# Attention values moved behind the MLP piece, and probability copies moved to the next step

## The chip, the cores and the metric

The kernel runs on one core of a Trainium2 chip. The metric is the time of one execution on the device, in microseconds (us). Below, PE is the matrix engine, PEld its weight loads, DVE the vector engine, ACT the scalar engine, POOL the GpSimd engine and SP the engine that issues most transfers. Each engine gets its own list of instructions in the order of the program; between engines, semaphores make a reader wait for its writer and a writer wait until a buffer is free.

## The reference

An attention of 2 batches, 8 heads, 768 positions and head size 64, in which a query sees four sink positions and a window of 128, is followed by two MLPs (512 to 2048 to 512) over the 1536 tokens:

```python
scores = scale * np.matmul(q, k.transpose(0, 1, 3, 2))
keep = is_sink | in_window
scores = np.where(keep, scores, -1000000000.0)
a = np.exp(scores - np.max(scores, axis=-1, keepdims=True))
a = a / (np.sum(a, axis=-1, keepdims=True) + 1e-09)
x = np.matmul(a, v)                       # heads joined to 512 columns
h = x @ w_in                              # first MLP
g = np.where(h > 0.0, h, alpha * (np.exp(np.minimum(h, 0.0)) - 1.0))
x = g @ w_out
h = x @ w_in2                             # second MLP
g = np.maximum(h, 0.0) + alpha2 * np.minimum(h, 0.0)
out = g @ w_out2
```

## The kernel before, in words

**Attention in steps.** The queries of a batch are cut into seven blocks of 110 (the last has 108). A unit is one or two blocks of one pair of heads; there are 32 units, and the loop `for s in range(nu + 2)` in `fast_path` runs 34 steps. A unit passes through three of them. In step s PE makes the scores of unit s (`scores`, line 521, tiles qk); DVE adds the mask and finds the maximum (line 529), ACT makes the exponentials (line 534), DVE the reciprocals of their sums (lines 544 and 547, tile st), and POOL multiplies by them (line 551, `normalised`). In the same step PE transposes the probabilities of unit s-1 (`transposed`, line 565, tiles t in PSUM), which DVE copies into SBUF (line 649, tiles pt; up to step 9 ACT copies the second block of a unit). And PE multiplies the values with the transposed probabilities of unit s-2 (`values`, line 586, tile x); ACT rounds the result to its high part xh (line 594), and DVE makes the remainder xl (line 596). xh and xl are the input of the first MLP.

**MLP pieces between.** All MLP products are made of three matmuls on high and low parts (`matmul3`, line 293). While attention runs, PE also takes one MLP piece a step from the list `fill`: an h piece (`g1`, 12 matmuls into one PSUM tile, evicted by two ACT operations at lines 325 and 326 and one DVE operation at 327, tile u; in the next step ACT makes gh at line 339 and POOL gl at line 340) or an o piece (`g2`, 12 matmuls, evicted by one ACT copy at line 359). The pieces have 220, 220, 328 and 440 columns; 32 of them are in the list, each with the first step at which it may run (`at_`). Where a step has no piece, two groups of four dummy matmuls (`keep_busy`, line 251, tile busy) stand in its place. What is left of the list runs after the loop.

**Weights.** Eight weight halves are decoded during attention, in the steps of `DS` (1, 3, 5, 7, 9, 10, 11, 12): two ACT operations (lines 267 and 268) at the end of the step before, four DVE operations (lines 270, 273, 276, 279) in the step, and one of ACT (line 283, wh) and one of DVE (line 285, wl) in the step after.

**Order.** Inside the loop the program sets the order by hand (`manual_schedule`): each engine gets its instructions in the order in which the Python code issues them. The tiles t, x, h, o and busy share four PSUM buffers (pool `ps`), taken in turn; qk has four of its own.

After the loop comes `mlp_rounds`, which does the rest of both MLPs with larger pieces.

Of the kernel before, what the change touches and what calls it, by code (L numbers as in the profile page):

```python
# [34 lines left out]
HP = H // 2  # L35
# [21 lines left out]
DS = [1, 3, 5, 7, 9, 10, 11, 12]  # L57
# [56 lines left out]
def attention_mlp2(  # L114
# [13 lines left out]
    nc = tc.nc  # L128
# [45 lines left out]
    def load_v(g, pool=None):  # L174
        b, z, hp = sgs[g]
        n = VCH[z] * 2 * D
        if pool:
            t = pool.tile([P, max(VCH) * 2 * D], F32, tag="vr", name=f"vr{g}", bufs=LB)
        else:
            t = room[:, HP * 2 * KTOT[0] + g * n :]  # L180
        nc.sync.dma_start(out=t[:, :n], in_=vc[b, hp, :, V0[z] : V0[z] + n])
        vals[g] = t
# [10 lines left out]
    def load_w(m, fc, io, raw=None):  # L193
        if raw is None:
            raw = rawp.tile([P, DM, 2], I32, tag="raw", name=f"wr{m}_{fc}_{io}")
        nc.sync.dma_start(
            out=raw, in_=weights[m][fc, io].bitcast(I32).rearrange("p (n t) -> p n t", t=2)
        )
        wraw[m, fc, io] = raw
# [18 lines left out]
    for i, most in enumerate((SINK, 0, WIN, 0)):  # L218
# [7 lines left out]
        out=flag_i, in0=int1[:, 2:3].bitcast(U32), scalar=0.5, in1=flag_m, op0=ALU.is_ge, op1=ALU.mult  # L226
# [6 lines left out]
        out=lims, in0=intf[:, :, 0], scalar=0.0, in1=intf[:, :, 1], op0=ALU.is_lt, op1=ALU.add  # L233
    )
    nc.vector.scalar_tensor_tensor(
        out=lims, in0=lims, scalar=4294967296.0, in1=intf[:, :, 0], op0=ALU.mult, op1=ALU.add
# [10 lines left out]
    def keep_busy(pool, tag, n):  # L247

        t = pool.tile([P, 512], F32, tag=tag, name=f"busy{next(ids)}")
        for _ in range(n):  # L250
            nc.tensor.matmul(t[:, :P], ident, ident, start=True, stop=True)  # L251
# [121 lines left out]
    def done(steps):  # L373
        for _ in steps:
            pass
# [87 lines left out]
    def make_mask(blk):  # L463
        o = sum(KW[i] for i in MASKS if i < blk)
        masks[blk] = mk = mask_t[:, o : o + KW[blk]]

        nc.vector.tensor_scalar(
            out=mk, in0=rels[blk].bitcast(U32), scalar1=win, scalar2=-NEG / SCALE,
            op0=ALU.is_ge, op1=ALU.mult,
        )  # L470

        nc.vector.scalar_tensor_tensor(
            out=mk[:, :SINK], in0=skey, scalar=ns, in1=mk[:, :SINK], op0=ALU.is_ge, op1=ALU.mult
        )
# [17 lines left out]
    def fast_path():  # L492
# [47 lines left out]
        def normalised(i):  # L540
            _, blks = units[i]
            n, c = NQ[blks[0]], len(blks)
            sb, st = soft[i]
            nc.vector.tensor_scalar(
                out=st[:n, 2, :c], in0=st[:n, 1, :c], scalar1=1.0e-9, scalar2=None, op0=ALU.add
            )
            nc.vector.reciprocal(st[:n, 3, :c], st[:n, 2, :c])  # L547
            for j, blk in enumerate(blks):
                w = KW[blk]
                for e in range(2):  # L550
                    nc.gpsimd.tensor_scalar(  # L551
                        out=sb[:n, j, e, :w], in0=sb[:n, j, e, :w], scalar1=st[:n, 3, j, e : e + 1],
                        scalar2=1.0, op0=ALU.mult, op1=ALU.mult,
                    )

        def transposed(i):
            _, blks = units[i]
            sb, _ = soft.pop(i)
            for j, blk in enumerate(blks):
                n, c, r = NQ[blk], NCH[blk], CR[blk]  # L560
                tp = ps.tile([P, 512], F32, tag="ps", name=f"t{i}_{blk}")
                for e in range(2):
                    for k in range(c):
                        o = (e * c + k) * n
                        nc.tensor.transpose(  # L565
                            tp[:r, o : o + n], sb[:n, j, e, k * r : k * r + r], ident[:n, :n]
                        )
                pt = at.tile([P, 4 * QB], F32, tag="pt", name=f"pt{i}_{blk}", bufs=PB)
                trans[i, blk] = pt
                yield pt[:r, : 2 * c * n], tp[:r, : 2 * c * n]  # L570

        def values(i):
            g, blks = units[i]
            b, z, hp = sgs[g]
            vr = vals[g]
            px = ps.tile([P, 512], F32, tag="ps", name=f"x{i}")
            o = 0
            for blk in blks:
                n, c, r = NQ[blk], NCH[blk], CR[blk]
                v0 = sum(NCH[SPLIT[z][0] : blk]) * 2 * D  # L580
                pt = trans.pop((i, blk))
                for e in range(2):
                    for k in range(c):
                        vs = v0 + (k * 2 + e) * D
                        p0 = (e * c + k) * n
                        nc.tensor.matmul(  # L586
                            px[e * D : e * D + D, o : o + n], vr[:r, vs : vs + D], pt[:r, p0 : p0 + n],
                            start=(k == 0), stop=(k == c - 1),
                        )
                o += n  # L590
            c0 = b * S + Q0[blks[0]]
            xh, xl = (x[:, hp, c0 : c0 + o] for x in xs)

            nc.scalar.copy(xh, px[:, :o])  # L594
            yield
            nc.vector.tensor_tensor(out=xl, in0=px[:, :o], in1=xh, op=ALU.subtract)  # L596


        nu = len(units)
        last_of = {g: i for i, (g, _) in enumerate(units)}  # L600
        fill = []
        first, second = [], []
        for j, (c0, n, t) in enumerate(TOK0[:-1]):
            at_ = last_of[t * HP + HP - 1] + 2
            first.append([(at_, lambda c0=c0, n=n, fc=fc: mlp.g1(0, c0, n, fc)) for fc in range(FG)])
            second.append([(at_, lambda c0=c0, n=n, d=d: mlp.g2(0, c0, n, 0, d)) for d in range(KC)])

# [15 lines left out]
        load_w(*ws[HP])  # L623
        decodes = {}
        gates = []
        for s in range(nu + 2):
            late = s - 1 in decodes
            if late:
                next(decodes[s - 1])
            for a in gates:  # L630
                done(a)
            gates = []
            if late:
                done(decodes.pop(s - 1))
            sc = scores(s) if s < nu else iter(())
            next(sc, None)
            vs = values(s - 2) if s >= 2 else iter(())
            next(vs, None)
            done(sc)
            done(vs)  # L640
            if s in decodes:
                next(decodes[s])
            take = 1 if fill and fill[0][0] <= s else 0
            after = fill.pop(0)[1]() if take else None
            if not take and s < nu:
                keep_busy(ps, "ps", BUSYN)
            if 1 <= s <= nu:
                for j, (out, in_) in enumerate(transposed(s - 1)):
                    (nc.scalar.copy if j and s <= DS[HP] else nc.vector.tensor_copy)(out, in_)  # L649
            if s < nu:  # L650
                normalised(s)
            if not take and s < nu:
                keep_busy(ps, "ps", BUSYN)
            if after:
                after = after()
                next(after)
                gates.append(after)
            if len([f for f in fill if f[0] <= s]) >= FILL_MAX:
                after = fill.pop(0)[1]()()
                next(after)  # L660
                gates.append(after)
            for blk, at_ in MS.items():
                if s == at_:
                    make_mask(blk)
            if s + 1 in DS:
                decodes[s + 1] = decode_w(at2, wa, *ws[DS.index(s + 1)])
                next(decodes[s + 1])
            if s in DS and WPRE <= DS.index(s) and DS.index(s) + 3 < len(ws):
                load_w(*ws[DS.index(s) + 3])
            if s < nu:  # L670
                g = units[s][0]
                if s == last_of[g] and HP <= g and g + LB < len(sgs):
                    load_kq(g + LB, at)
            if s >= 2:
                g = units[s - 2][0]
                if s - 2 == last_of[g] and HP <= g and g + LB < len(sgs):
                    load_v(g + LB, at)
# [97 lines left out]
    with tc.If(fast > 0) as cond:  # L775
        fast_path()
# [54 lines left out]
```

## Time and profile before

| | |
|---|---|
| Three timed runs | 662.41, 661.69 and 660.24 us, median 661.69 us |
| Profiled execution, from the first to the last instruction | 660.5 us; no time of its own is listed beside the three runs |
| Instructions | 9670 |
| Busy: PE / PEld / DVE / ACT / POOL | 633.7 / 526.6 / 435.9 / 315.7 / 204.4 us |
| Mean granted clock of PE | 0.986 |

Busy times are sums over the whole span; the loop of the attention steps fills about the first quarter of it. A row of the timeline gives the start, the duration, the engine, the line and operation, and in brackets how long the engine had been idle and for whom it waited. Rows of one engine overlap a little, since an instruction starts while the one ahead still writes; the time that an instruction takes from a busy engine is the distance from its start to the start of the next.

### The profile page before, as it was taken

What the parts mean: (1) busy time and instruction counts of PE and PEld (TensorE: products, weight loads), DVE (VectorE), ACT (ScalarE), POOL (GpSimd) and SP (SyncE); (2) the same over time, 40 slices, a digit from 0 to 9 for tenths busy, and PEclk for the clock granted to TensorE, in tenths of its full rate; (3) what the DMA queues carried; (4) which work ended last, traced back from release to release, by engine and by line L of the source; (5) the groups of instructions that cost most, each with busy time, mean ns of one, the idle gap of its engine ahead of it and who ended that gap; (6) DMA issues with size and microseconds to landing.
All of it is one profiled execution on the core that took longest, in us unless ns stands there. A gap on an engine that the chain in (4) does not pass through costs nothing.

```text
span 660.5 us, 9670 instructions
## 1 busy us (share of the span) xinstructions
PE 633.7 (96%) x3444; PEld 526.6 (80%) x3444; DVE 435.9 (66%) x927; ACT 315.7 (48%) x719; POOL 204.4 (31%) x253
## 2 busy tenths in 40 slices
PE   8986899999989899999999999999999999999996
PEld 7775688887977677888888888888888888888885
DVE  5877767655399997768465876694669673343332
ACT  4877466655588675647545733453524230110010
POOL 3354334434123321233215453332123312331130
PEclk9988799999999999999999999999999999999999
DMA  8574336500043343121112211212222000000112
GB/s 256 149 213 140 106 85 167 158 25 1 34 159 127 124 132 128 37 91 64 65 58 70 65 64 44 84 65 65 64 65 64 33 0 1 2 0 1 64 50 83
DMA packets 21659, 52.87 MB, mean 80 GB/s; under 512 B 2658, under 2 KB 9826, under 8 KB 21602
## 3 DMA queue, kind: packets, MB, share of 16 engines
q1 hardware_dynamic: 21024, 51.93, 25.8%
q8 instruction: 29, 0.48, 0.3%
q10 hardware_dynamic: 578, 0.24, 0.2%
q14 instruction: 28, 0.23, 0.1%
HBM read 49.01 MB, written 3.15 MB: 79 GB/s over the span
## 4 chain that ended last, share of the span: by engine, by line
PE 78%; DVE 13%; ACT 4%; issue 2%; POOL 1%; DMA 1%; DVEq 0%; ACTq 0%; SPq 0%; POOLq 0%
PE o L293 36%; PE h L293 34%; PE x L586 3%; DVE wx L276 3%; DVE wx L279 2%; ACT s L534 2%; PE t L565 2%; PE qk L521 2%; DVE wl L285 2%; DVE wx L273 1%; DVE wx L270 1%; DVE pt L649 1%; DVE u L327 1%; DVE acc L361 1%; PE busy L251 1%
## 5 line engine op out<-in xcount | busy, mean ns | idle before, releaser
L340 POOL TENSOR_TENSOR gl<-u,gh 128x512 fp32r<-128x512 f32 (+3 forms) x104 | 133.1, 1280 | 327.6 <-ACT gh L339 322.5
L293 PE MATMUL o<-gh,wh 128*128 128x512 f32 (+3 forms) x416 | 157.3, 380 | 5.5 <-DVE u L327 5.5
L293 PE MATMUL h<-xh,wh 128*128 128x512 f32 (+3 forms) x416 | 158.1, 380 | 1.2 <-ACT xh L594 1.2
L293 PE MATMUL o<-gl,wh 128*128 128x512 f32 (+3 forms) x416 | 156.3, 376 | 1.8 <-POOL gl L340 1.7
L293 PE MATMUL h<-xl,wh 128*128 128x512 f32 (+3 forms) x416 | 156.6, 376 | 0.1
L293 PE MATMUL h<-xh,wl 128*128 128x512 f32 (+3 forms) x416 | 156.4, 376 | 0.0
L293 PE MATMUL o<-gh,wl 128*128 128x512 f32 (+3 forms) x416 | 155.8, 375 | 0.0
L339 ACT CAST gh<-u 128x512 fp32r<-128x512 f32 (+3 forms) x104 | 60.9, 585 | 139.3 <-DVE u L335 114.2
L293 PEld LDWEIGHTS o<-gh,wh 128*128 128x128 f32 x416 | 78.4, 189 | 23.4 <-DVE u L327 8.4
L361 DVE TENSOR_TENSOR acc<-o,acc 128x512 f32<-128x512 f32 x72 | 49.2, 688 | 72.0 <-PE o L293 71.7
L293 PEld LDWEIGHTS h<-xh,wh 128*128 128x128 f32 x416 | 79.2, 190 | 16.9 <-ACT xh L594 1.3
L293 PEld LDWEIGHTS o<-gl,wh 128*128 128x128 f32 x416 | 78.8, 189 | 16.0 <-POOL gl L340 2.9
L293 PEld LDWEIGHTS h<-xl,wh 128*128 128x128 f32 x416 | 79.3, 191 | 13.6 <-DVE xl L596 0.4
L293 PEld LDWEIGHTS h<-xh,wl 128*128 128x128 f32 x416 | 79.4, 191 | 13.4
L293 PEld LDWEIGHTS o<-gh,wl 128*128 128x128 f32 x416 | 78.8, 189 | 13.5
L551 POOL TENSOR_SCALAR s<-s,st 110x250 f32<-110x250 f32 (+5 forms) x112 | 52.6, 487 | 92.3 <-DVE st L547 31.1
L283 ACT CAST wh<-wx 128x512 fp32r<-128x512 f32 x64 | 39.6, 619 | 65.6 <-DVE wx L279 31.7
L534 ACT ACTIVATE s<-s,st 110x250 f32<-110x250 f32 (+5 forms) x112 | 53.1, 477 | 27.1 <-DVE st L529 27.0
L331 DVE TENSOR_SCALAR u<-h,alpha_sb 128x512 f32<-128x512 f32 x48 | 35.9, 748 | 45.6 <-PE h L293 45.6
L279 DVE CUSTOM_DVE_ANT_0 wx<-wx,wq 128x1024 uint16<-128x1024 uint16 x64 | 59.2, 925 | 1.4
L276 DVE SCALAR_TENSOR_TENSOR wx<-wr,wx 128x512 int32<-128x512 int32 x62 | 56.6, 914 | 1.0
L285 DVE TENSOR_TENSOR wl<-wx,wh 128x512 fp32r<-128x512 f32 x64 | 46.8, 733 | 15.5 <-ACT wh L283 13.9
(56 smaller groups left out, 634.5 us busy)
## 6 DMA issues: line engine op xcount, KB each, us to landing
wr<-in_w_dram SPq DMA_DIRECT2D x62, 512.0 KB, 3.6
kq<-in_kq_dram SPq DMA_DIRECT2D x16, 237.0 KB, 4.4
vr<-in_vc_dram SPq DMA_DIRECT2D x8, 384.0 KB, 4.1
out_dram<-acc SPq DMA_DIRECT2D x12, 256.0 KB, 2.0
kq<-in_kq_dram SPq DMA_DIRECT2D x16, 180.0 KB, 3.8
vr<-in_vc_dram SPq DMA_DIRECT2D x8, 256.0 KB, 3.8
acc<-in_w_dram SPq DMA_DIRECT2D x2, 512.0 KB, 5.4
kq<-in_kq_dram SPq DMA_DIRECT2D x8, 110.0 KB, 3.4
```

Source lines behind the costliest of these rows:

```text
L276: nc.vector.scalar_tensor_tensor(out=x, in0=high, scalar=-0x40000000, in1=x, op0=ALU.bitwise_and, op1=ALU.bitwise_or)
L279: nc.vector.tensor_tensor(out=x, in0=x, in1=r, op=ALU.add)
L283: nc.scalar.copy(wh, xf)
L285: nc.vector.tensor_tensor(out=wl, in0=xf, in1=wh, op=ALU.subtract)
L293: nc.tensor.matmul(out, a, c, start=(i == 0), stop=(i == n - 1))
L331: nc.vector.tensor_scalar(out=u, in0=hp, scalar1=0.0, scalar2=alpha_sb[:, fc : fc + 1], op0=ALU.min, op1=ALU.mult,)
L339: nc.scalar.copy(gh, u)
L340: nc.gpsimd.tensor_tensor(out=gl, in0=u, in1=gh, op=ALU.subtract)
L361: nc.vector.tensor_tensor(out=a, in0=po, in1=a, op=ALU.add)
L534: nc.scalar.activation(sb[:n, j, e, :w], sb[:n, j, e, :w], AF.Exp, bias=st[:n, 0, j, e : e + 1], scale=-1.0, accum_out=st[:n, 1, j, e : e ...
L551: nc.gpsimd.tensor_scalar(out=sb[:n, j, e, :w], in0=sb[:n, j, e, :w], scalar1=st[:n, 3, j, e : e + 1], scalar2=1.0, op0=ALU.mult, op1=ALU. ...
L586: nc.tensor.matmul(px[e * D : e * D + D, o : o + n], vr[:r, vs : vs + D], pt[:r, p0 : p0 + n], start=(k == 0), stop=(k == c - 1),)
```

## The change

PE's work on values (line 586) goes behind the MLP piece of its step. The transposes of unit s-1 come after it, and their copies are the first thing that DVE (and ACT) get in step s+1. The eviction of the MLP piece and the normalisation come ahead of the values. Each MLP piece may start one step later than before (`+ 3` for `+ 2`).

```diff
-            at_ = last_of[t * HP + HP - 1] + 2
+            at_ = last_of[t * HP + HP - 1] + 3
...
+        copies = []
         for s in range(nu + 2):
+            for j, (out, in_) in enumerate(copies):
+                (nc.scalar.copy if j and s - 1 <= DS[HP] else nc.vector.tensor_copy)(out, in_)
+            copies = []
             late = s - 1 in decodes
...
             next(sc, None)
-            vs = values(s - 2) if s >= 2 else iter(())
-            next(vs, None)
             done(sc)
-            done(vs)
             if s in decodes:
                 next(decodes[s])
             take = 1 if fill and fill[0][0] <= s else 0
             after = fill.pop(0)[1]() if take else None
             if not take and s < nu:
                 keep_busy(ps, "ps", BUSYN)
-            if 1 <= s <= nu:
-                for j, (out, in_) in enumerate(transposed(s - 1)):
-                    (nc.scalar.copy if j and s <= DS[HP] else nc.vector.tensor_copy)(out, in_)
-            if s < nu:
+            if after:
+                after = after()
+                if s < nu: normalised(s)
+                next(after)
+                gates.append(after)
+            elif s < nu:
                 normalised(s)
+            vs = values(s - 2) if s >= 2 else iter(())
+            next(vs, None)
             if not take and s < nu:
                 keep_busy(ps, "ps", BUSYN)
+            if 1 <= s <= nu:
+                copies = list(transposed(s - 1))
+            done(vs)
+            after = None
             if after:
```

PE around steps 12 and 13, before (h0_220_2 and h0_220_3 are MLP pieces; the first number in the names t, qk, x and pt is the unit):

```order
L293 MATMUL h0_220_2_985<-xh_125,wl0_2_0_565 128x220
L565 MATMUL t10_4_998<-ident_103,s10_889 128x110 x4
L565 MATMUL t10_5_1005<-ident_103,s10_889 125x110 x4
L521 MATMUL qk12_4_0_1039<-kq10_723 110x256
L521 MATMUL qk12_4_1_1041<-kq10_723 110x256
L521 MATMUL qk12_5_0_1043<-kq10_723 110x250
L521 MATMUL qk12_5_1_1045<-kq10_723 110x250
L586 MATMUL x10_1051<-pt10_4_1003,vr9_806 64x110 x4
L586 MATMUL x10_1051<-pt10_5_1010,vr9_806 64x110 x4
L293 MATMUL h0_220_3_1070<-xh_125,wh0_3_0_728 128x220
```

and with the change:

```order
L293 MATMUL h0_220_2_1048<-xh_125,wl0_2_0_556 128x220
L586 MATMUL x10_1073<-pt10_4_1001,vr9_793 64x110 x4
L586 MATMUL x10_1073<-pt10_5_1007,vr9_793 64x110 x4
L565 MATMUL t11_6_1083<-ident_103,s11_953 121x108 x4
L521 MATMUL qk13_6_0_1099<-kq10_710 108x242
L521 MATMUL qk13_6_1_1101<-kq10_710 108x242
L293 MATMUL h0_220_3_1107<-xh_125,wh0_3_0_717 128x220
```

Before, only the four scores stand between the transposes of unit 10 and the values that need their copies. With the change a whole MLP piece stands there too, and the piece of 12 matmuls follows the scores directly.

DVE from step 21 into step 22, before (the lines 529 are the mask and maximum, st the reciprocals, u the eviction of an h piece):

```order
L529 ISA s21_1585,st21_1586<-qk21_3_1_1593,mask_129 110x244
L529 ISA st21_1586 110x1
L596 TENSOR_TENSOR xl_126<-x19_1599,xh_125 128x220
L649 COPY pt20_2_1630<-t20_2_1625 125x440
L649 COPY pt20_3_1637<-t20_3_1632 122x440
L544 TENSOR_SCALAR st21_1586<-st21_1586 110x4
L547 RECIPROCAL st21_1586<-st21_1586 110x4
L327 SCALAR_TENSOR_TENSOR u0_440_0_1645<-u0_440_0_1645,h0_440_0_1612 128x328
L529 ISA s22_1658,st22_1659<-qk22_2_0_1660,mask_129 110x250
```

and with the change, from step 22 into step 23:

```order
L529 ISA s22_1647,st22_1648<-qk22_3_1_1655,mask_129 110x244
L529 ISA st22_1648 110x1
L544 TENSOR_SCALAR st22_1648<-st22_1648 110x4
L547 RECIPROCAL st22_1648<-st22_1648 110x4
L327 SCALAR_TENSOR_TENSOR u0_440_0_1684<-u0_440_0_1684,h0_440_0_1665 128x328
L596 TENSOR_TENSOR xl_126<-x20_1690,xh_125 128x220
L629 COPY pt21_2_1705<-t21_2_1700 125x440
L629 COPY pt21_3_1711<-t21_3_1706 122x440
L529 ISA s23_1722,st23_1723<-qk23_2_0_1724,mask_129 110x250
```

The reciprocals, which wait for ACT's exponentials, and the eviction now stand ahead of xl, and the copies stand behind xl and ahead of the next step's first mask operation. ACT in the same place, with the change:

```order
L534 ACTIVATE s22_1647,st22_1648<-s22_1647,st22_1648 110x250 x2
L534 ACTIVATE s22_1647,st22_1648<-s22_1647,st22_1648 110x244 x2
L325 ACTIVATE u0_440_0_1684<-h0_440_0_1665 128x328
L326 ACTIVATE u0_440_0_1684<-u0_440_0_1684 128x328
L594 CAST xh_125<-x20_1690 128x220
L339 CAST gh0_440_0_1685<-u0_440_0_1684 128x328
```

Before, xh stood between the first and the second pair of exponentials; now it comes behind all four and behind the eviction.

## Rows read from the trace of the kernel before

**Rows 1.** Windows: us, then busy us and count of each engine, clock, DMA share, GB/s.

```profile
6.30:26.80 20.50, 19.74 (x180) 16.27 (x180) 16.44 (x72) 14.62 (x53) 7.16 (x16) 1.00 0.98 276
26.80:85.30 58.50, 48.18 (x397) 40.27 (x396) 43.41 (x147) 40.88 (x128) 23.51 (x42) 0.85 0.46 131
85.30:158.90 73.60, 72.39 (x649) 60.73 (x648) 47.83 (x203) 44.50 (x164) 32.00 (x66) 1.00 0.37 98
158.90:174.50 15.60, 14.63 (x90) 13.01 (x90) 3.40 (x9) 4.59 (x10) 3.18 (x4) 1.00 0.01 2
174.50:660.50 486.00, 474.05 (x2113) 391.92 (x2111) 323.10 (x488) 209.58 (x365) 135.59 (x100) 1.00 0.20 65
```

**Rows 2.** Waits, whole span: who waited for whom, total us, times, longest.

```profile
PE x L586 <- DVE pt L649: 10.8, 9, 3.5
```

**Rows 3.** Timeline of PE at a stall, steps 8 and 11 to 12.

```profile
43.50 1.03 PE L586 MATMUL x<-pt,vr 125*64 125x110 f32 x16 [2.01 <-DVE pt L649]
...
62.67 0.99 PE L586 MATMUL x<-pt,vr 121*64 121x108 f32 x8 [3.51 <-DVE pt L649]
...
63.94 0.42 PE L293 MATMUL h<-xl,wh 128*128 128x220 f32 x1
...
66.28 1.78 PE L565 MATMUL t<-ident,s 110*128 110x110 f32 x8
...
70.39 0.28 PE L293 MATMUL h<-xl,wh 128*128 128x220 f32 x1
70.50 0.27 PE L293 MATMUL h<-xh,wl 128*128 128x220 f32 x1
...
80.77 1.73 PE L521 MATMUL qk<-kq 64*110 64x256 f32 x8
```

**Rows 4.** Chain that ended last, steps 6 to 12: start, us, engine and line.

```profile
33.88 0.33 DVE s L529
34.26 1.09 ACT s L534 x4
35.35 0.23 ACT xh L594
35.58 0.97 ACT s L534 x4
...
68.27 1.05 DVE pt L649 x2
```

**Rows 5.** DVE by line, 26.8 to 85.3 us: busy, mean ns, idle before, releaser.

```profile
L649 DVE COPY pt<-t 125x440 f32<-125x440 f32 (+2 forms) x11 | 6.6, 608 | 3.3 <-PE t L565 3.3
...
L596 DVE TENSOR_TENSOR xl<-x,xh 128x220 fp32r<-128x220 f32 (+1 forms) x10 | 3.6, 364 | 6.6 <-ACT xh L594 6.6
```

**Rows 6.** Timeline of PE and ACT, steps 22 to 23.

```profile
111.71 1.09 PE L521 MATMUL qk<-kq 64*110 64x250 f32 x8
...
115.84 0.43 ACT L325 ACTIVATE u<-h 128x328 f32<-128x328 f32 x1
...
116.30 0.48 ACT L326 ACTIVATE u<-u 128x328 f32<-128x328 f32 x1
116.52 0.68 PE L521 MATMUL qk<-kq 64*110 64x250 f32 x4
```

**Rows 7.** Timeline of PE, step 26.

```profile
130.19 0.42 PE L293 MATMUL o<-gl,wh 128*128 128x328 f32 x1 [0.77 <-POOL gl L340]
```

**Rows 8.** Timeline, the last h piece of the attention steps.

```profile
163.03 0.54 ACT L325 ACTIVATE u<-h 128x440 f32<-128x440 f32 x1 [1.73 <-PE h L293]
...
163.60 0.57 ACT L326 ACTIVATE u<-u 128x440 f32<-128x440 f32 x1
...
164.27 0.61 DVE L327 SCALAR_TENSOR_TENSOR u<-u,h 128x440 f32<-128x440 f32 x1 [0.28 <-ACT u L326]
164.92 0.56 ACT L339 CAST gh<-u 128x440 fp32r<-128x440 f32 x1 [0.75 <-DVE u L327]
...
165.56 1.13 POOL L340 TENSOR_TENSOR gl<-u,gh 128x440 fp32r<-128x440 f32 x1 [3.29 <-ACT gh L339]
```

## The prediction, as it was made before the changed kernel ran

> **What bounds the kernel now.** Read the windows first [rows 1]. From 174.5 us on, after the attention steps, PE is busy 474.05 of 486.00 us, and the change touches nothing there: this part only moves as a whole. So the question is what ends the attention steps, and the windows cut them in four. In steps 0 to 4 (6.3 to 26.8 us) PE is busy 19.74 of 20.5 us. In steps 5 to 14 (26.8 to 85.3 us) it is busy 48.18 of 58.5 us, and the granted clock is 0.85. In steps 15 to 31 it is idle only 1.2 us of 73.6, in the end piece 1.0 of 15.6.
>
> The list of waits names the cause [rows 2]: PE waited nine times before line 586 for DVE's copies of the transposed probabilities, 10.8 us in all, 3.5 us at the longest. The timeline shows the two largest kinds [rows 3], 2.01 us at 43.50 and 3.51 us at 62.67. It also shows a second price: behind the long wait the matmuls of 220 columns last 0.42 us, the lower of the two clock levels (1.2 GHz), against 0.28 us at 70.39, the upper one (2.4 GHz). That is why the window has 0.85.
>
> Why is the copy late? DVE's copy stands behind four decode operations, and these behind xl, which waits for ACT's xh: in this window DVE sat idle 6.6 us before xl and 3.3 us before copies [rows 5]. So PE waits for DVE, DVE for ACT and PE in turn, and in 58.5 us DVE itself has only 43.41 us of work [rows 1].
>
> **The change part by part.** I go through the time of the profiled execution, 660.5 us; it lies 1.2 us under the median of the runs, 661.69 us, and I add the difference at the end.
>
> *Values behind the MLP piece, copies first in the next step.* Between a transpose and the values that need it PE now has the scores (about 1.0 us) and a piece of 12 matmuls (0.11 us from start to start [rows 3], about 1.4 us). Two copies take DVE 1.05 us [rows 4]. So the wait of [rows 2] goes wherever DVE is not behind by over about 1.3 us. xl no longer waits either, in steps where DVE is the late one, since PE and ACT are then ahead.
>
> Steps 0 to 4: the waits here are of the same kind, 0.76 us of idle PE in the window. I take **-0.7 us**; the end of the range is 0.
>
> Steps 5 to 14: with PE ahead, DVE sets the pace with its 43.41 us plus what it must still wait for. The new order keeps one wait: the reciprocals (st) need the last exponential. For two blocks, ACT starts 0.38 us behind DVE's first mask operation and needs 1.09 + 0.97 us [rows 4], while DVE has done its four operations after 1.36 us (four times about 0.34): about 1.3 us wait with hand-offs. Where decode operations stand between (steps 5, 7, 9 to 12) they fill it. Left are steps 6, 8 and 14 with 1.3 us and step 13, with one block, with 1.0 us: 4.9 us. Some 0.3 us for an eviction behind ACT's two operations in three steps, and 0.7 us for wl behind wh, come on top: 6.5 us. 43.4 + 6.5 = 49.9 us, against 58.5: **-8.6 us**. The bounds: all of DVE's idle time goes (-15.1 us), or the copies stay as late as they are (0). I take the sum, since it is made of DVE's own rows.
>
> *Step 5.* No piece is ready there any more, and dummies stand in its place; their two groups take about 2.0 us where the piece took 1.4. PE is not the late one in that window, so nothing, and 0.6 us if it is.
>
> *Pieces a step later.* The same 32 pieces run, but behind step 14 there is one more of 220 columns to do, in a stretch where PE is full: **+1.4 us**.
>
> *Steps 15 on.* PE's idle time there, 1.2 and 1.0 us [rows 1], includes the wait of 0.77 us for gl [rows 7]. The eviction now comes ahead of the copies, so gl comes earlier, and the waits for copies go: **-2.2 us** at most, and I take it. But the new order makes a ring over two engines: copies, first mask operation, four exponentials, eviction, xh, xl, copies. In the steps with h pieces of 328 columns its links take 1.05 + 0.38 + (1.09 + 0.97) + 0.43 + 0.48 + 0.23 + 0.36 = 5.0 us [rows 4 to 6], where PE's step takes 4.81 us, from 111.71 to 116.52 [rows 6]. That is 0.2 us in each of four steps. In the two steps ahead of them the o pieces have one ACT operation less, which makes the ring about 4.4 us; PE's step is shorter too by a narrower piece and narrower transposes, some 3.9 us (an estimate from the same rows): 1.0 us in two steps. Of all this 1 us is covered once, because copies may be late by that much. In the other steps the blocks are narrower or single, with shorter or fewer exponentials, and I take the ring as no longer than PE's step. **+0.8 us**; as bounds, 0 and 1.8.
>
> *The end.* The last h piece now stands in the last step, and the o pieces follow behind its eviction with only the values of one block (0.5 us) between. Their tenth to twelfth matmuls need gh and gl of it: 0.54 + 0.57 + 0.61 + 0.56 + 1.13 = 3.4 us [rows 8]. PE has 0.5 us of values and ten matmuls of 440 columns (about 0.2 us each) to do, 2.5 us: **+0.9 us**. In the two steps without scores a piece also waits for the PSUM buffer of the one before it, whose eviction takes 1.7 us against about 1.4 us of PE's other work: **+0.5 us** with hand-offs.
>
> Transfers: the loads of keys and values are issued at the same places of the loop; that of values waits for line 586, which comes some 1.5 to 2.5 us later in its step. They are made three pairs of heads ahead, and no row shows PE waiting for one. Nothing.
>
> Sum: -0.7 - 8.6 + 1.4 - 2.2 + 0.8 + 0.9 + 0.5 = **-7.9 us**, 652.6 us by the profiled execution and 653.8 us by the median. I say 654.0.
>
> **A rule against the change.** In the rows, PE waits for copies and never for a PSUM buffer: the four buffers of the pool are free in time [rows 2]. The change leaves the transposes in PSUM longer. The Trainium skill ("PSUM — Partial Sum Buffer", Summary: rules for kernel authors) says to evacuate promptly, and ("Perfetto Trace Analysis", Optimization Strategy) that a bubble that repeats can mean too little PSUM for the next tile. By that rule PE would trade the waits for copies for waits for buffers; the rival below works it out.
>
> **The rivals.**
>
> *Buffers.* An h piece takes the PSUM buffer of the last one and waits for its eviction. Between two of them PE has 0.96 + 0.9 + 1.0 us (values, transposes, scores), 2.9 us; the eviction takes 1.4 us by itself, but stands behind the exponentials and reciprocals. If it is late by 0.9 us in each of the eight later h pieces, that is 7.2 us in place of the 1.3 us counted: 660 us. For it: the ring above is long. Against it: the list of waits has no h matmul of the attention steps that waited for a buffer, and the eviction has 1.5 us to spare. Chance 0.08.
>
> *The lower clock stays: slower.* PE now idles a little in nearly every one of steps 5 to 14, up to 2 us where decode steps follow each other, and 2.01 us were enough for the lower level [rows 3]. At that level a two-block step takes 2.7 us of piece (from the end of the values at 63.6 to the transposes at 66.28), 1.7 of transposes, 1.7 of scores [rows 3] and about 1.0 of values, 7.0 us, a one-block step 5.3 us. Seven and three of them are 65 us, against 58.5 now; with the other terms, 668 us. Against it: in steps 0 to 4, with 0.76 us of idle PE spread over them, and in steps 15 to 31, with 1.2 us, the granted clock is 1.00 [rows 1]. It decides from about four such two-block steps on, since each costs 2 us over DVE's pace of 5. Chance 0.05. If the clock falls only behind one or two long waits, DVE's pace hides most of it: 1 to 3 us, 655 to 657 us, chance 0.13.
>
> *The copies are not first.* They stand behind xl, and that behind xh, which now comes after the eviction. If the copies come later by this than the MLP piece covers, half the waits stay in steps 5 to 14: 658 us, chance 0.10.
>
> *DVE never waits.* The exponentials are covered too, and the steps run at 45 us: 649 us, chance 0.06.
>
> **How the numbers follow.** The forecast has chance 0.58, with 651.5 to 656 us as its own range. 8 in 10 take in the fallen clock and part of the late copies: 650.5 to 658.5 us. About 0.3%, 2.0 us, is what a measurement can tell: under 659.7 us lie the forecast, the fallen clock, the late copies and the gain without waits, 0.87; the buffers are the same, 0.08; slower 0.05.
>
> **What would show it.** Right: in the waits of the changed profile line 586 behind the copies has under 5 us; the window of steps 5 to 14 is near 50 us with DVE busy over 85%; steps 15 to 31 keep their length within 1 us. Wrong: a wait of h or o matmuls for u (buffers), matmuls of 0.42 us through most of that window (clock), or steps of 5 us and more behind step 15 (the ring).

## The result, and the profile after

The changed kernel took 655.53 us (median of four runs, 655.21 to 656.02), the kernel before 661.91 us (four runs, 660.24 to 662.41). The ratio is 0.9914, 95% interval 0.9899 to 0.9929: 0.9% faster. The forecast was 654.0 us in a range of 650.5 to 658.5. The profiled execution has a span of 654.2 us, against 660.5: 6.3 us less, where the sum of the terms said 7.9.

First the windows of the changed kernel, cut at the same places of the program as [rows 1] (the starts of the first scores, and of those of steps 5 and 15, the end of step 31, the last instruction); columns as there.

```profile
5.60:25.40 19.80, 19.20 (x182) 16.14 (x182) 15.91 (x73) 14.45 (x52) 7.65 (x16) 1.00 1.06 291
25.40:75.80 50.40, 45.71 (x401) 36.79 (x400) 44.52 (x148) 38.98 (x126) 22.84 (x42) 0.93 0.55 154
75.80:149.40 73.60, 73.60 (x649) 59.90 (x648) 47.34 (x204) 44.95 (x166) 31.83 (x67) 1.00 0.37 98
149.40:168.00 18.60, 17.41 (x102) 15.04 (x102) 3.85 (x9) 5.84 (x12) 3.37 (x3) 1.00 0.01 1
168.00:654.20 486.20, 475.38 (x2113) 393.69 (x2111) 323.08 (x488) 209.47 (x365) 135.56 (x100) 1.00 0.20 65
```

| Stretch | before, us | after, us | difference | forecast |
|---|---|---|---|---|
| up to the first scores | 6.3 | 5.6 | -0.6 | 0 |
| steps 0 to 4 | 20.5 | 19.8 | -0.8 | -0.7 |
| steps 5 to 14 | 58.5 | 50.4 | -8.1 | -8.6 |
| steps 15 to 31 | 73.6 | 73.6 | 0.0 | -1.4 |
| the pieces left for the end | 15.6 | 18.6 | +3.0 | +2.8 |
| the rest | 486.0 | 486.2 | +0.2 | 0 |

(Differences are from unrounded starts. The forecast for the last three stretches is my terms sorted by place. Steps 15 to 31: idle PE -1.2, the ring +0.8, and -1.0 for the pieces, since one of 440 columns, 12 times 0.20 us, moved from there to the end and one of 220, 1.4 us, moved in. The end, with 102 matmuls in place of 90: +2.4 for that piece, +0.9 and +0.5 for its waits, and -1.0 of idle PE, together +2.8.)

The start is not the change's: the first scores came between 5.63 and 6.26 us in the profiles of this study, whatever the kernel.

Where [rows 2] had nine waits of line 586 for copies, 10.8 us, the list of waits of the changed kernel, from 0 to 170 us, has this for PE (who waited for whom, total us, times, longest):

```profile
PE h L293 <- DVE u L327: 3.1, 5, 1.2
...
PE x L586 <- DVE pt L629: 1.8, 2, 1.3
...
PE o L293 <- POOL gl L340: 0.7, 1, 0.7
PE o L293 <- DVE u L327: 0.7, 1, 0.7
```

Two waits for copies are left, 1.8 us. Five waits of h matmuls for line 327, the eviction that reads the PSUM buffer they want, are new, 3.1 us, and so is one of an o matmul, 0.7: six waits for evictions, 3.8 us. That is the buffers rival, in part.

DVE is what sets the pace of steps 5 to 14 now. Its lines in 25.4 to 75.8 us, which answer to [rows 5] (busy us, mean ns, idle before):

```profile
L629 DVE COPY pt<-t 125x440 f32<-125x440 f32 (+3 forms) x12 | 6.9, 586 | 0.0
...
L596 DVE TENSOR_TENSOR xl<-x,xh 128x220 fp32r<-128x220 f32 (+1 forms) x10 | 3.5, 352 | 0.0
```

The 3.3 us of idle time before copies and the 6.6 us before xl are both gone, and DVE is busy 44.52 of 50.40 us, 88%. Most of what it still waits for is one line of the list of waits, 26 to 86 us:

```profile
DVE st L544 <- ACT s L534: 6.0, 6, 1.1
```

The reciprocals wait for the last exponential, 1.0 to 1.1 us in steps 6, 8 and 14 and 0.8 in step 13 (4.1 us up to 75.8 us): the four steps that the prediction named, each a little under its 1.3 and 1.0.

The clock fell once in this execution. PE's timeline at that place, and above it at an earlier wait (start, us, and in brackets the wait; compare [rows 3]):

```profile
46.30 0.37 PE L293 MATMUL h<-xh,wh 128*128 128x220 f32 x1 [1.22 <-DVE u L327]
46.50 0.27 PE L293 MATMUL h<-xl,wh 128*128 128x220 f32 x1
...
57.61 0.60 PE L586 MATMUL x<-pt,vr 121*64 121x108 f32 x8 [1.25 <-DVE pt L629]
58.13 1.46 PE L565 MATMUL t<-ident,s 110*128 110x110 f32 x8
59.52 2.03 PE L521 MATMUL qk<-kq 64*110 64x256 f32 x8
62.15 0.55 PE L293 MATMUL h<-xh,wh 128*128 128x220 f32 x1 [0.60 <-DVE u L327]
62.50 0.42 PE L293 MATMUL h<-xl,wh 128*128 128x220 f32 x1
...
67.86 0.27 PE L293 MATMUL h<-xl,wh 128*128 128x220 f32 x1
```

The lower level came behind a wait of 1.25 us: matmuls of 220 columns take 0.42 us, and 0.27 again at 67.86. Behind the wait of 1.22 us at 46.30 they take 0.27 as before it, so the length of one wait does not tell whether the clock falls. The fall cost little, since DVE was the late one. A window around it shows DVE nearly without a gap:

```profile
53.80:70.40 16.60, 14.75 (x106) 11.56 (x105) 16.19 (x48) 11.65 (x37) 6.88 (x12) 0.79 0.58 171
```

Two of the four runs had a mean clock of 0.999, which leaves no room for such a stretch. They took 655.42 and 655.64 us; the profiled one, with 0.991, took 656.02.

### The profile page after: what moved, and what is told of

Its sections match the earlier page's. It is cut to its first block, busy times and chain, and to the rows that moved or that the text cites. A ratio compares the mean times of both kernels' runs of the same rounds, so it can differ in the third digit from the quotient of the medians.

```text
span 654.2 us, 9720 instructions
## 1 busy us (share of the span) xinstructions
PE 635.3 (97%) x3460; PEld 525.4 (80%) x3460; DVE 435.8 (67%) x927; ACT 315.2 (48%) x719; POOL 204.2 (31%) x253
## 4 chain that ended last, share of the span: by engine, by line
PE 78%; DVE 14%; ACT 3%; issue 3%; DMA 1%; POOL 1%; DVEq 0%; ACTq 0%; POOLq 0%; SPq 0%
PE o L293 37%; PE h L293 31%; PE x L586 3%; DVE wx L276 3%; PE qk L521 3%; PE t L565 3%; DVE wx L279 2%; DVE wl L285 2%; DVE wx L273 1%; DVE u L327 1%; DVE wx L270 1%; ACT s L534 1%; PE busy L251 1%; DVE s L529 1%; DVE acc L361 1%
## 5 line engine op out<-in xcount | busy, mean ns | idle before, releaser
L293 PEld LDWEIGHTS h<-xl,wh 128*128 128x128 f32 x416 | 78.8, 189 | 13.1
L285 DVE TENSOR_TENSOR wl<-wx,wh 128x512 fp32r<-128x512 f32 x64 | 47.9, 750 | 15.6 <-ACT wh L283 14.1
```

The lines of the kernel that those rows point to most:

```text
L285: nc.vector.tensor_tensor(out=wl, in0=xf, in1=wh, op=ALU.subtract)
L293: nc.tensor.matmul(out, a, c, start=(i == 0), stop=(i == n - 1))
```

## The experiments

My theory: the gain is PE's order (values behind the piece), the deferred copies and later pieces are worth nothing by themselves, and what is missing from the forecast lies behind step 14. The rivals were that the deferral does the work, that the ring over DVE and ACT is what holds steps 15 to 31, and that lower clocks eat part of the gain. The later pieces can't be left out of the change: a piece that stands ahead of the values of its step can't use what those values make. The first four runs share their runs of the kernel before (661.25 us), the last four theirs (660.57 us).

**e1: the later pieces alone.** The kernel before, with one number changed.

```diff
-            at_ = last_of[t * HP + HP - 1] + 2
+            at_ = last_of[t * HP + HP - 1] + 3
```

> The kernel before with one edit of the change, each MLP piece a step later. By the theory that PE's distance between transposes and values made the gain, the waits for copies stay: line 586 behind DVE's copies still near 11 us, and the time within 3 us of before (659 to 665 us); the wait of 1.2 us for xh goes, and one piece more remains to do late. By the rival that the later pieces made it, at least half the gain is here already: 658 us or less.

661.1 us, ratio 0.9991 (0.9974 to 1.0007). PE's waits for copies are what they were:

```profile
PE x L586 <- DVE pt L649: 11.1, 9, 2.6
```

So the third part of the change, alone, does nothing to the median that can be measured. (Three of its twelve runs took 658.0 to 658.1 us at a mean clock of 0.994, which no run of the kernel before shows; why is open.) In its profile it moves time: steps 5 to 14 take 55.7 us in place of 58.5, and all that is behind step 14 takes 578.0 in place of 575.2. One of its waits for copies bears on the clock:

```profile
54.67 1.03 PE L586 MATMUL x<-pt,vr 128*64 128x110 f32 x16 [2.15 <-DVE pt L649]
...
55.95 0.28 PE L293 MATMUL h<-xh,wl 128*128 128x220 f32 x1
```

Behind 2.15 us of idle PE the matmuls of 220 columns still take 0.28 us.

**e2: the deferral without PE's new order.** The changed kernel, with the values moved back ahead of the piece.

```diff
             done(sc)
+            vs = values(s - 2) if s >= 2 else iter(())
+            next(vs, None)
             if s in decodes:
...
-            vs = values(s - 2) if s >= 2 else iter(())
-            next(vs, None)
```

> The changed kernel with the values put back ahead of the MLP piece; the copies stay first in the next step. By the distance theory PE again has only the scores between transposes and values, and the copies come later than before, so the waits of line 586 for copies come back, 11 us or more, and the time is 662 to 672 us. By the rival that DVE's new order alone (reciprocals and eviction ahead of xl and copies) made the gain, it stays under 658 us.

670.32 us, ratio 1.0136 (1.0119 to 1.0153): slower than before. The list of waits, 0 to 170 us:

```profile
PE x L586 <- DVE pt L629: 17.9, 14, 2.6
```

With only the scores between a transpose and its values, a copy that comes a step later is a copy that PE waits for: 17.9 us against 10.8 [rows 2]. The deferral without PE's order is a loss, though this kernel keeps DVE's new order, with the reciprocals and the eviction ahead of xl; PE's order decides. In the profile the loss lies behind step 14: 587.1 us in place of 575.2, with waits for copies in steps 23 to 26 and at the end. Steps 5 to 14 take 55.3 us, between the 58.5 of before and the 50.4 of after.

**e3: PE's new order without the deferral.** The changed kernel, with each copy issued in the step of its transposes.

```diff
-                copies = list(transposed(s - 1))
+                for j, (out, in_) in enumerate(transposed(s - 1)):
+                    (nc.scalar.copy if j and s <= DS[HP] else nc.vector.tensor_copy)(out, in_)
```

> The changed kernel with the copies put back into the step of their transposes, ahead of the values' xl on DVE (they stay behind the eviction, since the values stay behind the MLP piece). By the distance theory the deferral itself is worth nothing: 654 to 657 us, waits of line 586 for copies under 4 us. By the rival that the copies must be first in the next step, 658 us or more.

656.02 us, ratio 0.9924 (0.9910 to 0.9938), beside 0.9914 (0.9899 to 0.9929) of the whole change: the intervals lie over each other, so the deferral is worth nothing measurable. Steps 5 to 14 take 51.62 us here and 50.40 there, one profile each. The copies still stand behind the reciprocals and the eviction here, where before they stood ahead of them; PE's order without that part of DVE's order was not run. The list of waits, 0 to 170 us, has the waits for evictions too:

```profile
PE h L293 <- DVE u L327: 4.1, 5, 1.6
```

So these do not come from transposes that stay longer in PSUM.

**e4: transposes straight behind the piece.** PE's order in after is piece, values, transposes, scores. Before, the transposes stood behind the piece. This kernel is after with piece, transposes, values, scores.

```diff
+            if 1 <= s <= nu:
+                copies = list(transposed(s - 1))
             vs = values(s - 2) if s >= 2 else iter(())
             next(vs, None)
             if not take and s < nu:
                 keep_busy(ps, "ps", BUSYN)
-            if 1 <= s <= nu:
-                copies = list(transposed(s - 1))
```

> The changed kernel with one swap on PE: transposes directly behind the MLP piece, values behind them. In steps 15 to 31 of the changed kernel PE is without idle time, yet from the MLP piece's first matmul to the next group it takes about 0.08 us longer than before, and the transposes to the scores 0.05 to 0.10 us, 2.6 us over 17 steps. By the theory that this is the price of a group that follows the piece or the values, the swap gives the first part back: 652 to 654.5 us, and 1.44 us from an o piece of 220 columns to the transposes where it now is 1.52. By the rival that the ring over DVE and ACT sets these steps, no gain: 655 to 657 us.

656.13 us, ratio 0.9928 (0.9916 to 0.9941): a miss, not faster than after. But its profile answers the question of steps 15 on. Here are windows of the sixteen steps 15 to 30 (same columns as [rows 1]), one for each kernel: before, e1, after, e4.

```profile
85.33:154.16 68.83, 67.73 (x617) 56.96 (x616) 45.18 (x193) 41.28 (x155) 29.06 (x61) 1.00 0.39 104
```

```profile
81.95:148.68 66.73, 66.40 (x617) 56.09 (x617) 44.70 (x192) 40.27 (x155) 27.92 (x60) 1.00 0.41 108
```

```profile
75.83:144.73 68.90, 68.90 (x618) 56.21 (x617) 44.99 (x195) 42.04 (x158) 29.17 (x63) 1.00 0.39 104
```

```profile
77.61:145.85 68.24, 67.02 (x619) 56.21 (x617) 44.35 (x194) 41.36 (x158) 28.30 (x61) 1.00 0.39 105
```

e1 is the fair comparison with after: the same matmuls and the same pieces in these steps (before has one h piece of 440 columns more there and one o piece of 220 fewer). PE has them done in 66.73 us with 0.33 idle; after needs 68.90 with none. At the same clock and without a wait, the new order takes 2.5 us more of PE's time. e4, with the transposes behind the piece again, is back to 67.02 busy. The place shows in the transposes' line among the groups by line of these windows (busy us, mean ns), of e1 and of after:

```profile
L565 PE MATMUL t<-ident,s 110*125 110x110 f32 (+4 forms) x105 | 13.3, 263 | 0.0
```

```profile
L565 PE MATMUL t<-ident,s 110*125 110x110 f32 (+4 forms) x105 | 14.5, 275 | 0.0
```

And in the timeline, at one step each, of before, after and e4 (start, us; PEld is the load of weights):

```profile
95.25 0.28 PE L293 MATMUL o<-gh,wl 128*128 128x220 f32 x1
95.28 0.59 PEld L565 LDWEIGHTS t<-ident,s 110*110 110x110 f32 x6
95.37 0.73 PE L565 MATMUL t<-ident,s 110*110 110x110 f32 x6
```

```profile
88.86 0.27 PE L293 MATMUL o<-gh,wl 128*128 128x220 f32 x1
89.06 0.63 PEld L586 LDWEIGHTS x<-pt,vr 110*64 110x64 f32 x12
89.06 0.84 PE L586 MATMUL x<-pt,vr 110*64 110x110 f32 x12
89.83 0.56 PEld L565 LDWEIGHTS t<-ident,s 110*110 110x110 f32 x6
89.83 0.78 PE L565 MATMUL t<-ident,s 110*110 110x110 f32 x6
90.54 0.82 PE L521 MATMUL qk<-kq 64*110 64x110 f32 x8
```

```profile
87.48 0.27 PE L293 MATMUL o<-gh,wl 128*128 128x220 f32 x1
87.52 0.59 PEld L565 LDWEIGHTS t<-ident,s 110*110 110x110 f32 x6
87.60 0.73 PE L565 MATMUL t<-ident,s 110*110 110x110 f32 x6
...
88.25 0.60 PE L586 MATMUL x<-pt,vr 121*64 121x108 f32 x8
```

From the start of a piece's last matmul to the next group it is 0.12 us before (95.25 to 95.37) and in e4, 0.20 in after. Six transposes occupy PE for 0.71 us behind values (89.83 to 90.54) and 0.65 behind a piece (87.60 to 88.25). In the quick seam the load of the transposes starts 0.08 to 0.09 us ahead of its matmul; in the slow ones load and matmul start together. Over the sixteen steps 15 to 30, from the start of a group to that of the next, transposes take 13.1 us in after and 11.9 in e1, and pieces 29.4 and 27.8, 0.1 a piece in every step. Scores take 0.6 us less in after, values the same, but 0.33 of theirs in e1 is waiting. That the load isn't ahead is what the rows show; why is not settled.

Why was e4 then no faster? Its profile started 0.6 us later, which is not the swap's, and it lost time in steps 0 to 4 and to waits in steps 23 to 25. Steps 0 to 4 took 21.2 us against 19.8; one transpose of step 2 waits 0.8 us there for POOL's products (the other 3.3 us of the first line below are in steps 5 to 14, which took no longer than after's). In steps 23 to 25 h pieces wait for the eviction. PE's waits, 0 to 170 us:

```profile
PE t L565 <- POOL s L551: 4.1, 5, 1.3
...
PE h L293 <- DVE u L327: 3.9, 7, 1.2
```

In steps 15 to 30 that second wait is 1.2 us in three. So the ring that the prediction feared is there, but shows only when PE is quick enough to run into it.

**e5: half as many dummies.** The changed kernel with `BUSYN = 2` in place of 4: dummies fill steps that have no piece, and if PE is not the late one there, fewer of them could only show what they do for the clock.

> The changed kernel with two dummy matmuls in a group instead of four. In steps 0 to 4 of the changed kernel PE is busy 19.2 of 19.8 us, half of it with dummies, DVE 15.9. By the theory that PE's dummies set the pace there, these steps shorten by 1 to 2.5 us, until DVE and ACT set it, with the clock at 1.00: 653 to 655 us. By the rival that the fewer dummies let the clock fall, matmuls at the lower level appear in steps 0 to 8 and the time is 656 us or more.

655.83 us, ratio 0.9927 (0.9906 to 0.9947): no gain, a miss. The window of steps 0 to 4, and the row of granted clocks in 40 slices of the page:

```profile
5.60:25.00 19.40, 17.46 (x143) 13.35 (x144) 15.92 (x73) 13.83 (x50) 7.71 (x16) 0.91 1.07 285
```

```profile
PEclk9999799999999999999999999999999999999999
```

There are 39 matmuls fewer than in after (143 against 182 in about the same window), and the clock is 0.91 where it was 1.00: six transposes in 1.36 us and scores in 1.45 us show the lower level in steps 1 to 3. The row of slices still has a 9 there; its 7 is the slice from 65.5 to 81.9 us, a second stretch at the lower level, in steps 13 and 14. The steps 0 to 4 themselves got 0.8 us shorter (18.98 against 19.76 from scores to scores), and steps 5 to 14 longer, 52.96 against 50.40. So what the shorter steps gave was lost again behind them. The rival, that the dummies keep the clock up, has its mechanism in this execution, but it does not explain the time: two of the six runs had a mean clock of 0.999, which leaves no room for such stretches, and took 655.10 and 655.52 us, no clear gain on after's 655.21 to 656.02. Why fewer dummies gave nothing there either is open.

**e6: the swap of e4 from step 6 on only.** The transposes go first only from step 6 on; steps 1 to 5 keep after's order.

```diff
+            if 6 <= s <= nu:
+                copies = list(transposed(s - 1))
             vs = values(s - 2) if s >= 2 else iter(())
...
-            if 1 <= s <= nu:
+            if 1 <= s <= min(5, nu):
                 copies = list(transposed(s - 1))
```

> The changed kernel with transposes ahead of values from step 6 on, and as it is before that. With the swap in all steps, steps 0 to 4 took 21.2 us instead of 19.8, PE waiting for POOL's products, and steps 15 to 31 gained 0.1 us a step but waited 1.4 us more for the eviction of h pieces. By the theory that both stand by themselves, the first loss goes and the rest stays: 654 to 655.3 us. By the rival that the swap gains nothing at all, 655.3 to 657 us.

654.57 us, ratio 0.9909 (0.9889 to 0.9929), as expected, though the interval lies over that of after, so the swap alone is no gain that can be told. Steps 0 to 4 are back at 19.72 us, steps 15 to 30 at 67.55, with the same waits for the eviction in them as e4's:

```profile
PE h L293 <- DVE u L327: 1.2, 3, 0.7
```

**e7: e6 with ACT copying the second block in every step.** This shortens the ring by half of its copies.

```diff
-                (nc.scalar.copy if j and s - 1 <= DS[HP] else nc.vector.tensor_copy)(out, in_)
+                (nc.scalar.copy if j else nc.vector.tensor_copy)(out, in_)
```

> As e6, and ACT copies the second block of every unit, where DVE does from step 11 on. By the ring theory (copies, mask, exponentials, eviction, xl, copies) DVE's link shortens by 0.53 us, the waits of h pieces for the eviction in steps 22 to 25 shrink from 1.4 us to under 0.5, and the time is about 1 us under e6. By the rival that ACT, with its exponentials, is the long link in these steps, its added copy makes the waits longer: e6 plus 0.5 to 2 us.

652.59 us, ratio 0.9879 (0.9857 to 0.9901), 2 us under e6, where I expected about 1 from the ring; five of its six runs are under all six of e6. The window of steps 15 to 30:

```profile
76.35:142.68 66.33, 66.33 (x619) 56.16 (x617) 38.43 (x183) 47.06 (x168) 28.71 (x62) 1.00 0.41 108
```

PE has no idle time left there (e6: 66.34 of 67.55), at the work of the old order (e1: 66.40). DVE's load fell from 44.0 to 38.4 us. So an engine that was busy only 65% of the time held PE up by its place in the ring, and a shorter link removed the wait: 1.2 us here. In the profiled executions (653.8 and 651.0 us) another 1.5 us came in steps 5 to 14, 50.37 against 51.87; what brought that was not singled out.

**e8: e7 with one more piece of the end taken into the steps.** `FILL_MAX = 11` in place of 13 makes a step take a second piece as soon as eleven are due.

> As e7, and one step (18) takes two MLP pieces, so that the last h piece comes a step earlier and three o pieces are left for the end instead of four. By the account of the end the wait of 0.73 us for gl before the o pieces goes, and some of the wait for the eviction before: 0.7 to 1.2 us under e7. By the rival that the second piece makes that step wait as much elsewhere, no difference.

650.81 us (650.54 to 651.35), ratio 0.9849 (0.9825 to 0.9873): the best of the study, clear of after's interval. The window of steps 15 to 30, and from the list of waits that for gl at the end:

```profile
76.46:143.98 67.52, 67.50 (x619) 56.96 (x617) 38.76 (x183) 48.10 (x167) 29.90 (x63) 1.00 0.40 106
```

```profile
PE o L293 <- POOL gl L340: 0.2, 1, 0.2
```

The step with two pieces is step 10, not 18 as I expected. From there on each piece comes a step earlier: steps 15 to 30 have one of 440 columns more and one of 220 fewer, which costs them 1.2 us (67.52 against 66.33), and the end loses a piece and most of the wait for gl (0.7 in after). It gave 1.8 us where I expected 0.7 to 1.2; which place gave the excess I did not single out.

## Why the prediction was right, and where it was 1.6 us off

- *Values behind the piece, steps 5 to 14: right.* Forecast -8.6, measured -8.1. DVE's pace, its own work plus the waits of st, was the right way to size it: 44.5 us of work (1.1 more than in [rows 1], all of it in line 285, 5.3 us in place of 4.2), and 4.1 us of waits in the four steps named. e2 and e3 show that PE's order, not the deferral, brings it. Not all of it, though: with the later pieces alone (e1) the stretch is already 2.8 us shorter, paid back behind step 14, and against e1 the new order leaves 5.3.
- *Steps 0 to 4: the number right, the cause only in part.* -0.8 against -0.7, but a wait for a copy of 0.57 us is left in step 2, and 0.3 of the gain lies in step 0, which has no transposes or values to move.
- *Dummies in step 5, transfers: nothing, as said.* Half the dummies (e5) measured the same.
- *The end: right in sum.* Two of its rows, in PE's timeline after:

```profile
149.85 0.47 PE L293 MATMUL h<-xh,wh 128*128 128x440 f32 x1 [0.38 <-DVE u L327]
...
160.29 0.47 PE L293 MATMUL o<-gl,wh 128*128 128x440 f32 x1 [0.73 <-POOL gl L340]
```

The wait for a PSUM buffer is 0.38 us (I said 0.5), that for gl 0.73 (0.9).
- *"Steps 15 on": the step that failed.* It said that the waits for copies go, -2.2 us, "and I take it". They went: PE is busy 73.60 of 73.60 us. But I took PE's own work to be the same in any order, and it isn't: the same groups took 2.5 us more in sixteen steps (e1 against after), and that swallowed the gain. It makes 1.4 of the 1.6 us that are missing; the others are 0.5 in steps 5 to 14 and 0.4 at the end and beyond, less the 0.6 of the early start, which was luck, and 0.1 in steps 0 to 4. My sign for this place, a length within 1 us of before, could not show it: the length stayed at 73.6 us, where my terms summed to -1.4.
- *The ring, +0.8: the wrong cause of a time that came.* Steps 22 to 24 took 5.0 us each, as its links added up to (step 25, with one block of scores, 4.6), but with no wait of PE in them: PE itself needed that long. That the two agree is luck. e4 and e6, with a quicker PE, show the ring's wait (1.2 us), and e7 takes it away.
- *The buffers rival: in part.* 3.8 us of waits for the eviction took the place of most of the 10.8 us for copies, nearly all of it in steps where DVE set the pace anyway. The Trainium skill's rule ("PSUM — Partial Sum Buffer", Summary: rules for kernel authors) to evacuate promptly points at these waits; as a verdict on this change it is not borne out, since copying at once (e3) measured the same as copying a step later and left 4.1 us of such waits.
- *The clock rivals:* in the profile it fell once, behind 1.25 us, and stayed hidden behind DVE. The time lies in their 655 to 657 us, but two runs with a mean clock of 0.999 took 655.42 and 655.64 us, so the fall does not make it. In e1 and e2, whose waits for copies stayed, the granted clock of steps 5 to 14 is 0.88.

## What to carry to other kernels

When an in-order engine waits for a copy of its own product, look first for work of its own to put between the two; when the copy is issued matters less, and moving the copy alone can make it worse. When you forecast a reorder on a full engine, price the seams: the same instructions may take longer behind another neighbour, here 0.15 us a step. Behind a wait that is removed, follow the ring of the other engines, and shorten the link that a less busy engine can take.

## What the runs showed of the hardware that I had not expected

- The same transposes occupy PE for 0.65 us behind a piece and 0.71 behind values (six of them), and a group that follows a piece starts 0.12 or 0.20 us after the start of its last matmul, at the same granted clock of 1.00. In the slower cases the load of weights starts no earlier than its matmul.
- 1.25 us of idle PE (57.6 us, after) was followed by the lower clock level, 1.22 us (46.3 us, after) and 2.15 us (54.7 us, e1) were not. The 2.01 us of [rows 3], which the prediction took as enough, do not make a rule.
- With two of four dummies taken out of each group the profiled execution was at the lower level in steps 1 to 3, with PE still busy 17.46 of 19.40 us; two of the six runs had a mean clock of 0.999.
